# Narrowing float64 weights by integer bit operations on VectorE and ScalarE in a fused attention and gated feed-forward kernel

## The chip, the cores and the metric

One core of one Trainium2 chip runs the whole program. The metric is the device time of one launch in microseconds, the lower the better. The kernel before took 374.76 us (median of three runs, 373.27 to 375.42).

## The reference

```
a = S1 @ x, b = S2 @ x per token and head           # x is q or k, r = 8
phi(x) = outer(a, b), flattened to 64 features
kv = sum_s phi(k) v^T,  z = sum_s phi(k)
attn = (phi(q) @ kv) / (phi(q) . z + 1e-6)           # batch 4, heads 4, seq 1088, head_dim 32
x = attn as 4352 tokens x 128
out = (sigmoid(x @ w_gate) * (x @ w_val)) @ w_out    # d_ff 1536
```

q, k, v are float32. S1, S2 and the three weight matrices are float64: numpy's division and product by a float64 scalar make them so. They reach the chip as pairs of 32-bit words (low, high), and the kernel itself makes float32 of them.

## The kernel before, in words

The feed-forward part (called moe in the code) works on chunks of 512 tokens (`tok_chk`, eight of 512 and one of 256) and on twelve blocks of 128 hidden units (`NJ` = 12). For one chunk and one block, `w1` (L281) issues a **wave**: the gate and the value product into one PSUM tile (L292), a sigmoid on ScalarE (ACT, L300), and, emitted with the next wave, the product of the two on VectorE (DVE, L305, `glu`). `w2` (L246) multiplies the result of a block with w_out into the accumulator `moeout` (L252), some two waves later. There are 102 waves: twelve for each of the eight chunks of 512 tokens, and six of two blocks each for the last chunk.

The attention of batch 0 is computed ahead of the first wave as far as the first chunk needs it. All else of the attention (groups of matmuls for the feature maps `ab`, `kps`, `kv`, `den`, `num`) is put between the waves by `slot` (L319): a slot is one group and then one or two waves. The order on TensorE (PE), DVE, ACT and GpSimd (POOL) is the order in which the program text emits the instructions; each engine works through its own queue in that order. Loads are issued by SyncE (SP), each queued behind the waits of the ones ahead of it.

PSUM is tight: waves and the `aps` half of `ab` share two buffers (`psm`). Where an `ab` stands between two waves, the second of them takes the buffer of the first, and so waits for that wave's `glu` on DVE.

The first chunk is special: its twelve waves each need a new block of weights, and a block is narrowed just ahead. `load_w` (L135) loads two blocks of all three matrices into one `raw` buffer; `narrow_w(j)` (L156) narrows block j of the three matrices at once, 128 partitions x 384 values, into `w_sb`. Blocks 0 to 2 are narrowed ahead of wave 0, and wave j of the first chunk emits `narrow_w(j + 3)` ahead of its matmuls (L288). `narrow` (L81) makes, for one block:

- on DVE four integer operations: `head` (sign, exponent, upper mantissa; L94, L98), `power` (L101) and `ex` (L104);
- on ACT one copy of the low words to float, `rest` (L109);
- on POOL six operations: rest x power, + head, two comparisons of the exponent, their sum, and the last product, which writes `w_sb` (L110, L111, L113, L114, L117, L118).

The same `narrow` also treats S1 and S2 (`sr`, 128 x 64 values) at the start of the program; the feature matrices `sk`, `sa` and `sb` (L226 to L232) come from it, and every matmul of the attention needs one of them.

Of the kernel before, what the change touches and what calls it, by code (L numbers as in the profile page):

```python
# [8 lines left out]
F32 = mybir.dt.float32  # L9
I32 = mybir.dt.int32  # L10
U32 = mybir.dt.uint32
I64 = mybir.dt.int64
ALU = mybir.AluOpType
ACTF = mybir.ActivationFunctionType
MUL = ALU.mult
# [5 lines left out]
def kernel(  # L21
# [12 lines left out]
    nc = tc.nc  # L34
# [6 lines left out]
    NJ = DFF // P  # L41
    assert DM == H * D == P and D == 32 and R == 8 and S % 32 == 0

    T = S // 32
# [7 lines left out]
    const = ctx.enter_context(tc.tile_pool(name="const", bufs=1))  # L52
    ld = ctx.enter_context(tc.tile_pool(name="ld", bufs=2))
    sbA = ctx.enter_context(tc.tile_pool(name="sbA", bufs=2))
    raw = ctx.enter_context(tc.tile_pool(name="raw", bufs=3))
    sbN = ctx.enter_context(tc.tile_pool(name="sbN", bufs=2))
    sbG = ctx.enter_context(tc.tile_pool(name="sbG", bufs=6))

    psm = ctx.enter_context(tc.tile_pool(name="psm", bufs=2, space=bass.MemoryType.PSUM))
# [14 lines left out]
    q_chk = [(0, 9), (9, TP - 9)]  # L74
    T0 = 2 * q_chk[0][1]

    # float64 arrays arrive as int64 bit patterns, float32 ones as they are.
    wide = S1.dtype == I64
    assert all((a.dtype == I64) == wide for a in (S2, moe_w_gate, moe_w_val, moe_w_out))

    def narrow(out, bits):  # L81
        """out = the nearest float32 of the float64 in bits, pairs of words (low, high).

        Below float32's normal range it gives 0, beyond its largest value inf or NaN."""
        n, m = out.shape[1:]
        lo, hi = bits[:, :, :, 0].bitcast(U32), bits[:, :, :, 1]

        def tmp(dt, tag):
            return sbN.tile([P, 3, P], dt, tag=tag, name=tag)[:, :n, :m]

        head, power, ex = tmp(I32, "head"), tmp(I32, "power"), tmp(I32, "ex")
        rest, ok, big = tmp(F32, "rest"), tmp(F32, "ok"), tmp(F32, "big")
        # head: sign, exponent and the 20 mantissa bits of the high word, as a float32.
        nc.vector.tensor_scalar(  # L94
            out=head, in0=hi, scalar1=3, scalar2=0x3FFFFFF8,
            op0=ALU.logical_shift_left, op1=ALU.bitwise_and,
        )
        nc.vector.scalar_tensor_tensor(  # L98
            out=head, in0=hi, scalar=-0x40000000, in1=head, op0=ALU.bitwise_and, op1=ALU.bitwise_or
        )  # L100
        nc.vector.tensor_scalar(  # L101
            out=power, in0=head, scalar1=-0x800000, scalar2=None, op0=ALU.bitwise_and
        )
        nc.vector.tensor_scalar(  # L104
            out=ex, in0=hi, scalar1=20, scalar2=0x7FF,
            op0=ALU.logical_shift_right, op1=ALU.bitwise_and,
        )
        # rest: the low word's share, low * 2^-52 * (+-2^exponent).
        nc.scalar.activation(out=rest, in_=lo, func=ACTF.Copy, scale=2.0**-52)  # L109
        nc.gpsimd.tensor_tensor(out=rest, in0=rest, in1=power.bitcast(F32), op=MUL)  # L110
        nc.gpsimd.tensor_tensor(out=rest, in0=rest, in1=head.bitcast(F32), op=ALU.add)  # L111
        # The factor for the exponent: 0 too small, 1 in range, huge too large.
        nc.gpsimd.tensor_scalar(out=ok, in0=ex, scalar1=896.5, scalar2=None, op0=ALU.is_ge)  # L113
        nc.gpsimd.tensor_scalar(  # L114
            out=big, in0=ex, scalar1=1150.5, scalar2=3e38, op0=ALU.is_ge, op1=MUL
        )
        nc.gpsimd.tensor_tensor(out=ok, in0=ok, in1=big, op=ALU.add)  # L117
        nc.gpsimd.tensor_tensor(out=out, in0=rest, in1=ok, op=MUL)  # L118

    sr = const.tile([P, 2, D], F32, tag="sr", name="sr")  # L120
    sr_in = const.tile([P, 2, D, 2], I32, tag="sr_in", name="sr_in") if wide else None
    for n, s_ in enumerate((S1, S2)):
        rows = bass.AP(tensor=s_.tensor, offset=s_.offset, ap=[[0, P // R], [D, R], [1, D]])
        if wide:
            nc.scalar.dma_start(
                out=sr_in[:, n].rearrange("p d w -> p (d w)"), in_=rows.bitcast(I32)
            )
        else:
            nc.scalar.dma_start(out=sr[:, n], in_=rows)

    # w_sb[:, 0] = w_gate, [:, 1] = w_val (rows: model), [:, 2] = w_out (rows: within block j).
    w_sb = const.tile([P, 3, NJ, P], F32, tag="w_sb", name="w_sb")
    w_in = {}

    def load_w(n):  # L135
        j0, j1 = 2 * n, 2 * n + 2
        cs = slice(j0 * P, j1 * P)
        if wide:
            w_in[n] = raw.tile([P, 3, 2, P, 2], I32, tag="w_in", name="w_in")
        for i, src in enumerate((moe_w_gate, moe_w_val)):  # L140
            if wide:
                nc.sync.dma_start(
                    out=w_in[n][:, i].rearrange("p j m w -> p (j m w)"),
                    in_=src[:, cs].bitcast(I32),
                )
            else:
                nc.sync.dma_start(
                    out=w_sb[:, i, j0:j1].rearrange("p j m -> p (j m)"), in_=src[:, cs]
                )
        src = moe_w_out[cs, :].bitcast(I32) if wide else moe_w_out[cs, :]  # L150
        nc.sync.dma_start(
            out=w_in[n][:, 2].rearrange("p j m w -> p j (m w)") if wide else w_sb[:, 2, j0:j1],
            in_=src.rearrange("(j p) m -> p j m", p=P),
        )

    def narrow_w(j):  # L156
        n, jj = divmod(j, 2)
        if wide:
            narrow(w_sb[:, :, j, :], w_in[n][:, :, jj])
        if jj == 1 and n + 3 < NJ // 2:  # L160
            load_w(n + 3)

    # Column 32 t + i of a head is its token i T + t: 32 partitions a head, T tokens each.
    def load_rows(src, b, tag, parts=((0, T),)):
        t = ld.tile([P, T, D], F32, tag=tag, name=tag)
        for t0, t1 in parts:
            nc.sync.dma_start(
                out=t[:, t0:t1, :],
                in_=bass.AP(
                    tensor=src.tensor,  # L170
                    offset=src[b, 0].offset + t0 * D,
                    ap=[[T * D, P], [1, (t1 - t0) * D]],
                ),
            )
        return t
# [17 lines left out]
    k_t[0] = load_rows(k, 0, "k", halves)  # L193
    q_t[0] = load_rows(q, 0, "q", halves)
    v_t[0] = load_v(0)
    for n in range(3):
        load_w(n)

    def load_batch(b):
# [4 lines left out]

    load_batch(1)

    if wide:
        narrow(sr, sr_in)
    ones = const.tile([P, 32], F32, tag="ones")
    nc.vector.memset(ones, 1.0)  # L210

    sig0 = const.tile([P, 1], F32, tag="sig0")
    nc.scalar.activation(out=sig0, in_=ones[:, :1], func=ACTF.Sigmoid)
    ident = const.tile([P, P], F32, tag="ident")
    make_identity(nc, ident)

# [7 lines left out]
    for n, inner in enumerate(([[1, R], [0, R]], [[0, R], [1, R]])):  # L224
# [3 lines left out]
        t = const.tile([P, R, R], F32, tag=f"s{n}", name=f"s{n}")  # L228
        nc.scalar.copy(
            out=t, in_=bass.AP(tensor=st_.tensor, offset=st_.offset, ap=[list(st_.ap[0])] + inner)  # L230
# [6 lines left out]
    for n in range(2):  # L237
        t = const.tile([P, H, 32], F32, tag=f"zb{n}", name=f"zb{n}")
# [42 lines left out]
    def w1():  # L281

        ci = moe["ci"]
        t0, tw = tok_chk[ci]
        jn = TCH // tw
        j0 = moe["w"] * jn
        wv = psm.tile([P, 2, TCH], F32, tag="wave", name="wave")
        if ci == 0 and j0 + 3 < NJ:  # L288
            narrow_w(j0 + 3)
        for which in range(2):  # L290
            for jj in range(jn):
                nc.tensor.matmul(  # L292
                    out=wv[:, which, jj * tw : (jj + 1) * tw],
                    lhsT=w_sb[:, which, j0 + jj, :],
                    rhs=xT[:, t0 : t0 + tw],
                    start=True,
                    stop=True,
                )
        sg = sbG.tile([P, TCH], F32, tag="sg", name="sg", bufs=3)
        nc.scalar.activation(out=sg, in_=wv[:, 0], func=ACTF.Sigmoid)  # L300

        # Emitted with the next wave, so that the vector engine need not wait for the sigmoid.
        def glu():
            g = sbG.tile([P, TCH], F32, tag="g", name="g")
            nc.vector.tensor_tensor(out=g, in0=wv[:, 1], in1=sg, op=MUL)  # L305
            moe["todo"].append((ci, j0, jn, g.rearrange("p (j t) -> p j t", j=jn)))

        moe["gate"] = glu
        moe["w"] += 1
        if j0 + jn == NJ:  # L310
            moe["ci"] += 1
            moe["w"] = 0
# [41 lines left out]
    def turn_q(b, n):  # L354
        if b >= B:
            return
        if n == 0:
            qT_of[b] = sbA.tile([P, TP, 2, 32], F32, tag="qT", name="qT")
        t0, tn = q_chk[n]
        nc.vector.transpose(  # L360
            out=qT_of[b][:, t0 : t0 + tn].rearrange("p t c s -> p (t c s)"),
            in_=q_t[b][:, 2 * t0 : 2 * (t0 + tn)].rearrange("p t d -> p (t d)"),
        )
# [225 lines left out]
    invert()  # L589
    divide()  # L590
    narrow_w(2)
    turn_q(0, 1)

    def r_group(a_of, b_of):
# [83 lines left out]
```

## Time and profile before

| what | value |
|---|---|
| time, median of three runs | 374.76 us (373.27 to 375.42) |
| span of the profiled execution | 371.5 us |
| the profiled execution's own time | not listed apart; its span lies 3.3 us under the median |
| PE busy | 323.0 us (87%) |
| DVE busy | 172.5 us (46%) |
| POOL busy | 86.2 us (23%) |
| ACT busy | 80.6 us (22%) |

How to read it: the span goes from the first to the last instruction of the program, and what the runs take beyond it lies around the program. Busy shares are means over the whole span. Here they hide two stages: in the first 107 us PE has gaps and POOL is always busy; after that PE is always busy and POOL never. So the stages have to be looked at one by one. "Granted clock" is what TensorE got: 1.00 is 2.4 GHz and 0.50 is 1.2 GHz.

### The profile page before, as it was taken

The page shows a single profiled execution, that of the slowest core. Times are in us where ns is not written, and L with a number is a line of the kernel's source. Part 1 is how long each engine was busy: PE and PEld are TensorE (multiplying, and loading weights), DVE is VectorE, ACT ScalarE, POOL GpSimd, SP SyncE. Part 2 cuts the span into 40 slices and gives each one's busy share as a digit, 9 for nine tenths or more (in the row PEclk, how much of TensorE's full clock was granted, in tenths as well). Part 3 has the DMA queues.
Part 4 walks back from the last instruction along what each step waited for, and adds up shares of the span by engine and source line. Part 5 has one row for each costly group of instructions (what it writes and reads, how often), then busy time and mean ns, then how long its engine had stood idle before and what let it go on. Part 6 is the DMA issues. An engine that isn't in the chain of part 4 may idle for free.

```text
span 371.5 us, 3973 instructions
## 1 busy us (share of the span) xinstructions
PE 323.0 (87%) x1552; PEld 139.3 (37%) x1552; DVE 172.5 (46%) x294; ACT 80.6 (22%) x140; POOL 86.2 (23%) x86
## 2 busy tenths in 40 slices
PE   0735876675779999999999999999999999999994
PEld 0312222221323344343343434444444444444583
DVE  1886565699237654545742454222222322322321
ACT  3112112111212122221222111212222122221220
POOL 1179999999950000000000000000000000000000
PEclk9986788788699999999999999999999999999998
DMA  8960353110011000100001001000100100010010
GB/s 197 349 169 12 135 150 59 60 52 10 18 48 28 2 1 2 22 8 0 2 3 27 0 0 19 11 0 0 29 1 0 30 0 0 11 19 0 2 28 14
DMA packets 25587, 14.09 MB, mean 38 GB/s; under 512 B 19168, under 2 KB 22752, under 8 KB 25568
## 3 DMA queue, kind: packets, MB, share of 16 engines
q1 hardware_dynamic: 25280, 13.77, 14.7%
q8 instruction: 12, 0.20, 0.2%
q10 hardware_dynamic: 288, 0.07, 0.1%
q14 instruction: 7, 0.06, 0.1%
HBM read 11.60 MB, written 2.23 MB: 37 GB/s over the span
## 4 chain that ended last, share of the span: by engine, by line
PE 70%; POOL 21%; DVE 4%; issue 1%; DMA 1%; ACT 1%; POOLq 0%; ACTq 0%
PE wave L292 42%; PE moeout L252 22%; POOL big L114 5%; POOL ok L113 4%; POOL rest L110 3%; POOL rest L111 3%; POOL w_sb L118 3%; POOL ok L117 3%; DMA sr_in<-in_S_dram 1%; PE aps L414 1%; PE dps L515 1%; PE nps L550 1%; PE kps L372 1%; PE kvz L451 1%; DVE kp L391 1%
## 5 line engine op out<-in xcount | busy, mean ns | idle before, releaser
L292 PE MATMUL wave<-xT,w_sb 128*128 128x512 f32 (+1 forms) x432 | 200.8, 593 | 19.4 <-POOL w_sb L118 9.8
L305 DVE TENSOR_TENSOR g<-wave,sg 128x512 f32<-128x512 f32 x102 | 70.0, 686 | 130.9 <-ACT sg L300 130.9
L292 PEld LDWEIGHTS wave<-xT,w_sb 128*128 128x128 f32 x432 | 83.6, 197 | 120.9 <-issue 85.9
L252 PE MATMUL moeout<-g,w_sb 128*128 128x512 f32 (+1 forms) x216 | 109.6, 600 | 0.6 <-DVE g L305 0.6
L300 ACT ACTIVATE sg<-wave 128x512 f32<-128x512 f32 x102 | 60.8, 596 | 204.8 <-PE wave L292 204.8
L252 PEld LDWEIGHTS moeout<-g,w_sb 128*128 128x128 f32 x216 | 38.8, 194 | 44.1 <-issue 40.1
L433 DVE TENSOR_TENSOR qp<-bps,asb 128x576 f32<-128x576 f32 (+1 forms) x16 | 11.4, 720 | 22.0 <-PE bps L414 17.0
L109 ACT ACTIVATE rest<-w_in 128x384 f32<-128x384 uint32 x12 | 6.5, 553 | 61.9 <-POOL w_sb L118 61.9
L114 POOL TENSOR_SCALAR big<-ex 128x384 f32<-128x384 int32 (+1 forms) x13 | 18.6, 1434 | 0.8
L414 PE MATMUL aps<-qT,s 32*64 32x288 f32 (+1 forms) x128 | 13.2, 482 | 5.3 <-DVE g L305 2.9
L110 POOL TENSOR_TENSOR rest<-rest,power 128x384 f32<-128x384 f32 (+1 forms) x13 | 13.8, 1061 | 16.9 <-ACT rest L109 16.9
L372 PE MATMUL kps<-kT,sk 64*32 64x288 f32 x64 | 4.4, 548 | 14.5 <-DVE kT L348 14.5
L113 POOL TENSOR_SCALAR ok<-ex 128x384 f32<-128x384 int32 (+1 forms) x13 | 15.3, 1179 | 0.0
L391 DVE TENSOR_TENSOR kp<-kab 128x576 f32<-128x576 f32 (+2 forms) x20 | 14.5, 766 | 0.0
L111 POOL TENSOR_TENSOR rest<-rest,head 128x384 f32<-128x384 f32 (+1 forms) x13 | 13.4, 1028 | 1.0
L414 PE MATMUL bps<-qT,s 32*64 32x288 f32 (+1 forms) x128 | 13.0, 481 | 0.0
L117 POOL TENSOR_TENSOR ok<-ok,big 128x384 f32<-128x384 f32 (+1 forms) x13 | 12.4, 953 | 1.1
L118 POOL TENSOR_TENSOR w_sb<-rest,ok 128x384 f32<-128x384 f32 x12 | 12.3, 1029 | 0.9
L414 PEld LDWEIGHTS aps<-qT,s 32*64 32x64 f32 x128 | 4.0, 150 | 18.4 <-DVE qT L360 6.2
L424 ACT COPY asb<-aps 128x576 f32<-128x576 f32 (+1 forms) x16 | 9.8, 610 | 5.2 <-PE aps L414 3.7
L560 DVE TENSOR_TENSOR xT<-nps,rb 128x576 f32<-128x576 f32 (+1 forms) x8 | 5.8, 724 | 7.7 <-PE nps L550 7.6
L101 DVE TENSOR_SCALAR power<-head 128x384 int32<-128x384 int32 (+1 forms) x13 | 8.9, 681 | 0.5
(53 smaller groups left out, 118.2 us busy)
## 6 DMA issues: line engine op xcount, KB each, us to landing
v<-in_v_dram SPq DMA_DIRECT2D x16, 144.0 KB, 7.4
k<-in_k_dram SPq DMA_DIRECT2D x3, 544.0 KB, 6.3
q<-in_q_dram SPq DMA_DIRECT2D x3, 544.0 KB, 7.8
w_in<-in_moe_w_gate_dram SPq DMA_DIRECT2D x6, 256.0 KB, 4.1
w_in<-in_moe_w_val_dram SPq DMA_DIRECT2D x6, 256.0 KB, 4.3
w_in<-in_moe_w_out_dram SPq DMA_DIRECT2D x6, 256.0 KB, 5.6
out_dram<-o_sb SPq DMA_DIRECT2D x20, 64.0 KB, 2.0
k<-in_k_dram SPq DMA_DIRECT2D x1, 288.0 KB, 3.0
```

The costliest lines, as they stand in the source:

```text
L110: nc.gpsimd.tensor_tensor(out=rest, in0=rest, in1=power.bitcast(F32), op=MUL)
L111: nc.gpsimd.tensor_tensor(out=rest, in0=rest, in1=head.bitcast(F32), op=ALU.add)
L113: nc.gpsimd.tensor_scalar(out=ok, in0=ex, scalar1=896.5, scalar2=None, op0=ALU.is_ge)
L114: nc.gpsimd.tensor_scalar(out=big, in0=ex, scalar1=1150.5, scalar2=3e38, op0=ALU.is_ge, op1=MUL)
L117: nc.gpsimd.tensor_tensor(out=ok, in0=ok, in1=big, op=ALU.add)
L118: nc.gpsimd.tensor_tensor(out=out, in0=rest, in1=ok, op=MUL)
L252: nc.tensor.matmul(out=moe["acc"][:, :tw], lhsT=w_sb[:, 2, j, :], rhs=g[:, jj, :tw], start=(j == 0), stop=(j == NJ - 1),)
L292: nc.tensor.matmul(out=wv[:, which, jj * tw : (jj + 1) * tw], lhsT=w_sb[:, which, j0 + jj, :], rhs=xT[:, t0 : t0 + tw], start=True, stop=True,
L300: nc.scalar.activation(out=sg, in_=wv[:, 0], func=ACTF.Sigmoid)
L305: nc.vector.tensor_tensor(out=g, in0=wv[:, 1], in1=sg, op=MUL)
L391: nc.vector.tensor_tensor(out=KP[b][:, h, j0:j1].rearrange("p j (i l) -> p j i l", i=R), in0=bass.AP(tensor=a0.tensor, offset=a0.offset, a ...
L414: nc.tensor.matmul(out=dst[64 * c : 64 * c + 64, m, : 32 * tn], lhsT=sx[rows, :], rhs=qT_of[bb][rows, t0 : t0 + tn, c, :], start=True, sto ...
```

## The change

The steps of `narrow` are other ones, they run on other engines, and its last step is emitted later.

```diff
-    raw = ctx.enter_context(tc.tile_pool(name="raw", bufs=3))
-    sbN = ctx.enter_context(tc.tile_pool(name="sbN", bufs=2))
+    raw = ctx.enter_context(tc.tile_pool(name="raw", bufs=4))
+    sbN = ctx.enter_context(tc.tile_pool(name="sbN", bufs=4))
...
-        head, power, ex = tmp(I32, "head"), tmp(I32, "power"), tmp(I32, "ex")
-        rest, ok, big = tmp(F32, "rest"), tmp(F32, "ok"), tmp(F32, "big")
...
+        cap, head, tail = tmp(I32, "cap"), tmp(I32, "head"), tmp(I32, "tail")
+        nc.vector.tensor_scalar(
+            out=cap.bitcast(F32), in0=hi.bitcast(F32), scalar1=122880.0, scalar2=-122880.0,
+            op0=ALU.min, op1=ALU.max,
+        )
+        nc.vector.tensor_scalar(
+            out=head, in0=cap, scalar1=3, scalar2=0x3FFFFFF8,
+            op0=ALU.logical_shift_left, op1=ALU.bitwise_and,
+        )
+        nc.vector.scalar_tensor_tensor(
+            out=head, in0=cap, scalar=-0x40000000, in1=head, op0=ALU.bitwise_and, op1=ALU.bitwise_or
+        )
+        nc.scalar.activation(out=tail, in_=lo, func=ACTF.Copy, scale=2.0**-29)
+        nc.scalar.activation(out=cap.bitcast(F32), in_=cap.bitcast(F32), func=ACTF.Square)
+        nc.gpsimd.tensor_tensor(out=head, in0=head, in1=tail, op=ALU.add)
+
+        def last():
+            nc.vector.scalar_tensor_tensor(
+                out=out, in0=cap.bitcast(F32), scalar=1.265625 * 2.0**-30, in1=head.bitcast(F32),
+                op0=ALU.is_ge, op1=MUL,
+            )
+
+        return last
...
-            nc.scalar.dma_start(
+            nc.sync.dma_start(
                 out=sr_in[:, n].rearrange("p d w -> p (d w)"), in_=rows.bitcast(I32)
             )
...
-        if jj == 1 and n + 3 < NJ // 2:
-            load_w(n + 3)
+        if jj == 1 and n + 4 < NJ // 2:
+            load_w(n + 4)
...
-    for n in range(3):
+    for n in range(4):
         load_w(n)
...
-    if wide:
-        narrow(sr, sr_in)
...
     nc.scalar.activation(out=sig0, in_=ones[:, :1], func=ACTF.Sigmoid)
+    if wide:
+        narrow(sr, sr_in)()
...
-        if ci == 0 and j0 + 3 < NJ:
-            narrow_w(j0 + 3)
+        if ci == 0:
+            if j0 + 3 < NJ:
+                narrow_w(j0 + 3)
+            narrow_last(j0 + 1)
...
     narrow_w(2)
+    narrow_last(0)
```

For one block there are now three operations on DVE (`cap`, and `head` twice), two on ACT (`tail`, and the square of `cap`), one integer add on POOL, and a last operation on DVE that writes `w_sb`. `narrow_w` keeps that last one, and `narrow_last(j)` emits it: for block j + 1 with wave j, so two waves after the block's first steps.

On DVE around wave 0 (`xT` is the attention's output, `w_in` and `w_sb` the weights before and after narrowing, `g` the output of `glu`), in the program before:

```order
L560 TENSOR_TENSOR xT<-nps,rb 128x2x9x32
L94 TENSOR_SCALAR head<-w_in 128x384
L98 SCALAR_TENSOR_TENSOR head<-w_in,head 128x384
L101 TENSOR_SCALAR power<-head 128x384
L104 TENSOR_SCALAR ex<-w_in 128x384
L360 STREAM_TRANSPOSE qT<-q 128x512
```

and in the changed one, whose line numbers differ:

```order
L568 TENSOR_TENSOR xT<-nps,rb 128x2x9x32
L94 TENSOR_SCALAR cap<-w_in 128x384
L99 TENSOR_SCALAR head<-cap 128x384
L103 SCALAR_TENSOR_TENSOR head<-cap,head 128x384
L113 SCALAR_TENSOR_TENSOR w_sb<-cap,head 128x3x128
L368 STREAM_TRANSPOSE qT<-q 128x512
```

So the write of `w_sb` has come from POOL to DVE, and the one for wave 0 stands behind the first three steps of block 2.

On ACT around the first waves (`asb` is the copy of the `aps` half of a group of the attention, `sg` the sigmoid), before:

```order
L109 ACTIVATE rest<-w_in 128x384
L300 ACTIVATE sg<-wave 128x512
L424 COPY asb<-aps 128x2x256
L109 ACTIVATE rest<-w_in 128x384
L300 ACTIVATE sg<-wave 128x512
```

and now:

```order
L107 ACTIVATE tail<-w_in 128x384
L108 ACTIVATE cap<-cap 128x384
L308 ACTIVATE sg<-wave 128x512
L432 COPY asb<-aps 128x2x256
L107 ACTIVATE tail<-w_in 128x384
L108 ACTIVATE cap<-cap 128x384
L308 ACTIVATE sg<-wave 128x512
```

Each sigmoid now has the square of a block's `cap` ahead of it, which waits for that block's three steps on DVE.

SP's queue begins, in the changed program, with S1 and S2, which ACT issued before:

```order
L125 DMA sr_in<-in_S_dram 128x1x64 x2
L173 DMA k<-in_k_dram 128x576
L173 DMA k<-in_k_dram 128x512
L173 DMA q<-in_q_dram 128x576
L173 DMA q<-in_q_dram 128x512
```

Behind these come v, now four pairs of blocks of weights instead of three, and then the loads of batch 1.

## Rows read from the trace of the kernel before

**Rows 1.** The chain that ended last, share of the span by engine

```profile
PE 70%; POOL 21%; DVE 4%; issue 1%; DMA 1%; ACT 1%; POOLq 0%; ACTq 0%
```

**Rows 2.** Stretches: busy of PE, PEld, DVE, ACT, POOL; granted clock; DMA share, GB/s

```profile
27.79:107.44 79.65, 53.70 (x272) 18.44 (x273) 51.95 (x77) 14.52 (x28) 76.27 (x66) 0.78 0.22 63
90.00:100.00 10.00, 7.96 (x54) 2.85 (x55) 4.91 (x9) 2.11 (x4) 9.54 (x9) 0.50 0.00 0
107.44:371.50 264.06, 258.96 (x1062) 115.91 (x1062) 103.62 (x172) 60.01 (x101) 0.00 (x0) 1.00 0.06 9
```

**Rows 3.** Timeline of POOL, first block and last write: start, us, what

```profile
20.51 1.00 POOL L110 TENSOR_TENSOR rest<-rest,power 128x384 f32<-128x384 f32 x1 [9.86 <-ACT rest L109]
21.59 1.19 POOL L111 TENSOR_TENSOR rest<-rest,head 128x384 f32<-128x384 f32 x1
...
24.08 1.50 POOL L114 TENSOR_SCALAR big<-ex 128x384 f32<-128x384 int32 x1
...
106.39 0.99 POOL L118 TENSOR_TENSOR w_sb<-rest,ok 128x384 f32<-128x384 f32 x1
```

**Rows 4.** Timeline of PE: the gate and value products of three waves

```profile
27.79 3.78 PE L292 MATMUL wave<-xT,w_sb 128*128 128x512 f32 x4 [1.81 <-POOL w_sb L118]
...
107.44 1.98 PE L292 MATMUL wave<-xT,w_sb 128*128 128x512 f32 x4 [2.43 <-POOL w_sb L118]
...
137.32 1.88 PE L292 MATMUL wave<-xT,w_sb 128*128 128x512 f32 x4
```

**Rows 5.** Waits from 28 to 107.5: total us, times, longest

```profile
ACT rest L109 <- POOL w_sb L118: 61.9, 10, 7.3
...
PE wave L292 <- POOL w_sb L118: 9.8, 5, 3.3
...
PE wave L292 <- ACT asb L424: 9.6, 4, 4.4
```

**Rows 6.** Timeline of the queues of ACT and SP: S1 and S2, then q

```profile
0.71 1.28 ACTq L125 DMA_DIRECT2D sr_in<-in_S_dram  x2
...
1.64 1.09 SPq L167 DMA_DIRECT2D q<-in_q_dram  x2
```

**Rows 7.** Transfers: KB each, median us from issue to landing

```profile
q<-in_q_dram SPq DMA_DIRECT2D x1, 288.0 KB, 5.6
...
sr_in<-in_S_dram ACTq DMA_DIRECT2D x2, 32.0 KB, 3.8
```

**Rows 8.** Timeline of DVE, ahead of wave 0

```profile
11.92 0.73 DVE L360 STREAM_TRANSPOSE qT<-q 128x576 f32<-128x576 f32 x1
...
18.32 0.54 DVE L94 TENSOR_SCALAR head<-w_in 128x384 int32<-128x384 int32 x1
18.90 0.56 DVE L98 SCALAR_TENSOR_TENSOR head<-w_in,head 128x384 int32<-128x384 int32 x1
19.49 0.36 DVE L101 TENSOR_SCALAR power<-head 128x384 int32<-128x384 int32 x1
...
20.81 1.11 DVE L98 SCALAR_TENSOR_TENSOR head<-w_in,head 128x384 int32<-128x384 int32 x1
21.96 1.03 DVE L101 TENSOR_SCALAR power<-head 128x384 int32<-128x384 int32 x1
...
23.37 0.33 DVE L506 COPY zb<-ndps 64x4 f32<-64x4 f32 x2
...
26.81 0.76 DVE L560 TENSOR_TENSOR xT<-nps,rb 128x576 f32<-128x576 f32 x1
```

**Rows 9.** DVE groups by shape: busy us, mean ns, idle before

```profile
L101 DVE TENSOR_SCALAR power<-head 128x384 int32<-128x384 int32 x12 | 8.7, 722 | 0.4
L98 DVE SCALAR_TENSOR_TENSOR head<-w_in,head 128x384 int32<-128x384 int32 x12 | 7.7, 645 | 0.4
L104 DVE TENSOR_SCALAR ex<-w_in 128x384 int32<-128x384 int32 x12 | 6.5, 546 | 4.9 <-POOL big L114 4.9
L94 DVE TENSOR_SCALAR head<-w_in 128x384 int32<-128x384 int32 x12 | 6.5, 541 | 1.4 <-POOL rest L111 1.4
```

More of the change, by code (lines that the diff above doesn't have):

```diff
@@ L89, in tmp @@
             return sbN.tile([P, 3, P], dt, tag=tag, name=tag)[:, :n, :m]
-        head, power, ex = tmp(I32, "head"), tmp(I32, "power"), tmp(I32, "ex")
-        rest, ok, big = tmp(F32, "rest"), tmp(F32, "ok"), tmp(F32, "big")
+        cap, head, tail = tmp(I32, "cap"), tmp(I32, "head"), tmp(I32, "tail")
         nc.vector.tensor_scalar(
-            out=head, in0=hi, scalar1=3, scalar2=0x3FFFFFF8,
+            out=cap.bitcast(F32), in0=hi.bitcast(F32), scalar1=122880.0, scalar2=-122880.0,
[3 more added lines that the diff above has]
+            out=head, in0=cap, scalar1=3, scalar2=0x3FFFFFF8,
             op0=ALU.logical_shift_left, op1=ALU.bitwise_and,
@@ L98, in narrow @@
         nc.vector.scalar_tensor_tensor(
-            out=head, in0=hi, scalar=-0x40000000, in1=head, op0=ALU.bitwise_and, op1=ALU.bitwise_or
+            out=head, in0=cap, scalar=-0x40000000, in1=head, op0=ALU.bitwise_and, op1=ALU.bitwise_or
         )
[L101 to L118, printed above, removed]
+        nc.scalar.activation(out=tail, in_=lo, func=ACTF.Copy, scale=2.0**-29)
[7 more added lines that the diff above has]
+        return last
     sr = const.tile([P, 2, D], F32, tag="sr", name="sr")
@@ L128 @@
         else:
-            nc.scalar.dma_start(out=sr[:, n], in_=rows)
+            nc.sync.dma_start(out=sr[:, n], in_=rows)
     w_sb = const.tile([P, 3, NJ, P], F32, tag="w_sb", name="w_sb")
@@ L154, in load_w @@
         )
+    narrowed = {}
     def narrow_w(j):
@@ L158, in narrow_w, with narrow_last @@
         if wide:
-            narrow(w_sb[:, :, j, :], w_in[n][:, :, jj])
-        if jj == 1 and n + 3 < NJ // 2:
-            load_w(n + 3)
+            narrowed[j] = narrow(w_sb[:, :, j, :], w_in[n][:, :, jj])
+        if jj == 1 and n + 4 < NJ // 2:
+            load_w(n + 4)
+    def narrow_last(j):
+        if j in narrowed:
+            narrowed.pop(j)()
     def load_rows(src, b, tag, parts=((0, T),)):
```

## The prediction

> **What bounds the kernel now.** I read the chain that ended last first. It lies on PE for 70% of the span and on POOL for 21% [rows 1]; an engine that does no matmul holds a fifth of the time. The busy time by stretch says where [rows 2]. From 107.44 us on, PE is busy 258.96 of 264.06 us at a granted clock of 1.00 and POOL does nothing: that part is PE's own work. Between 27.79 and 107.44, POOL is busy 76.27 of 79.65 us, PE only 53.70, at a mean clock of 0.78.
>
> POOL's timeline tells why. Its first step for a block of weights starts at 20.51 and its last write of `w_sb` at 106.39 [rows 3]: twelve blocks of six operations, (106.39 + 0.99 - 20.51) / 12 = 7.24 us a block. Wave 0 starts at 27.79 and wave 11, the last one that needs a new block, at 107.44, and both are released by POOL's write of `w_sb` [rows 4]. So the first chunk's waves come at POOL's pace, and what else was late there was late through it: ACT waited 61.9 us for POOL to give its buffers back, PE 9.8 us directly, and 9.6 us for copies on ACT that stood behind that wait [rows 5].
>
> So the time is: start of wave 11, plus 264 us in which PE is always busy, plus the edges. The change can only move the start of wave 11, since the slots behind it keep their order.
>
> **The sum: up to wave 0.** S1 and S2 now go first on SP. Their two issues took ACT 1.28 us, and SP issued the first half of q at 1.64 [rows 6]. The median transfer of S1 and S2 took 3.8 us, that half of q 5.6 [rows 7]; so q landed at about 7.2, where DVE turned it only at 11.92 [rows 8], behind work that needs `sr` from POOL. With the two issues ahead of it on SP, q lands at about 8.5. S1 and S2 are there by 0.7 + 1.3 + 3.8 = 5.8 and need one small add on POOL instead of six steps, so q is the later of the two, and DVE turns it 11.92 - 8.5 = 3.4 us earlier. Bounds: nothing, if the loads behind it set the pace of the attention's first steps; and 4.7 us, if q lands as early as before. I take 3.5, since the rows on q are the nearest.
>
> The narrowing of blocks 0 and 1 stands on DVE ahead of the attention's last steps: from 18.32 to 23.37, 5.05 us for eight operations, two of which were stretched while POOL worked [rows 8]. Now there are six, with POOL idle until the first add: 0.54 + 0.36 + 0.56 and small gaps make 1.55 us a block, 3.1 for two, a gain of 2.0. `xT` is then finished at 26.81 + 0.76 - 5.5 = 22.1. But wave 0 no longer waits for POOL: its `w_sb` is written by DVE behind three steps of block 2, 1.55 + 0.65 us. Wave 0 starts at 24.3, that is 3.5 us earlier.
>
> **Wave 0 to wave 11.** DVE was busy 51.95 us there [rows 2]. Of it go the four old operations of ten blocks, 0.722 + 0.645 + 0.546 + 0.541 = 2.45 us each [rows 9], so 24.5. What stays is 27.5 us of attention and `glu`. New: nine blocks (3 to 11) of three steps at 1.6 us (each between its value alone, as above, and its mean beside POOL, since one add is left) = 14.4, and eleven last operations, which are of the form of L98, at 0.65 = 7.2. Together 49 us of DVE work in place of 52: DVE does as much as before, without POOL's pace over it.
>
> PE's own work there: behind wave 11 nine slots of the same kind took 137.32 - 107.44 = 29.88 us with PE never idle, 3.32 us each [rows 4]; eleven slots are 36.5 us at 2.4 GHz, 46.8 us at a clock of 0.78, 73 at 1.2 GHz. So DVE and PE are about equally loaded, and they wait for each other: a wave behind an `ab` needs the `glu` of the wave before, that `glu` the sigmoid, and the sigmoid now has a `cap` square ahead of it on ACT, which waits for three steps on DVE. These waits no row shows. Below, they are nothing; above, the stage is PE's 73 us at half clock. The nearest row is PE's 9.6 us behind ACT's copies [rows 5]; I take 7, as ACT no longer waits for POOL. 49 + 7 = 56 us in place of 79.65.
>
> POOL's add, between 1.0 and 1.2 us [rows 3] for a block that now takes some 5, is hidden; ACT's second operation lies in its idle time (busy 14.52 of 79.65 us [rows 2]) but for the order just named. The fourth `raw` buffer moves three loads ahead of batch 1's, whose first use is behind wave 2: hidden. The loads of batch 2 keep their place behind the weights, which now get their buffers earlier: hidden too.
>
> Wave 11 starts at 24.3 + 56 = 80.3 instead of 107.44: 27 us less. The span of 371.5 becomes 344.4, and the median of 374.76, which lies 3.3 us above it, **347.7 us**.
>
> **A rule that speaks against it.** One row of L98 took 0.56 us with POOL idle and the next 1.11 beside it, L101 0.36 and 1.03 [rows 8]. The Trainium skill ("Advanced Engine Details and Errata", VectorE Performance Modes) says that the second Vector port is shared with GpSimd, so that such instructions block each other; the trace agrees. The new last operation is of just this kind and it runs on the engine that now sets the pace. If every add holds DVE for all of its own time, that is 11 x 1.1 = 12 us where my sum has some 2.5 (0.65 against 0.56, 1.6 against 1.46): 347.7 + 9.5 = 357.2 us. It is a rival below.
>
> **The rivals.**
> 1. *DVE alone sets the pace, nothing waits.* Wave 11 at 24.3 + 49 = 73.3, or 71 with shorter operations: 338 to 341 us. For it: DVE's queue has work in nearly every slot. Against: the chain from `glu` to `glu` through PSUM.
> 2. *PE stays at 1.2 GHz.* In the stretch from 90 to 100 the granted clock was 0.50 although PE was busy 7.96 of 10 us [rows 2]. At half clock throughout, wave 11 starts at 24.3 + 73 = 97.3: 364.6 us. Against: PE works more densely than before, and it got 0.78 even so. By the skill's "TensorE: Matmul & The Clock Gate" (Part 1), idle time throttles and activity releases the clock, which fits the 1.00 of the unbroken stretch.
> 3. *The shared port*, as above: 357.2 us.
> 4. *Nothing is gained ahead of the attention* (S1 and S2 on SP delay k, q and v as much as they help): 351 us.
> 5. *Slower: the int32 add.* No row shows an add of two int32 tensors on POOL. The nearest are a float add of 1.19 us and an operation with an int32 input of 1.50 [rows 3]; a price below these changes nothing, as it is hidden. If it took a path many times as long, POOL would set the pace again: its adds start near 16.3 (18.32 - 3.5 + 1.5), so it decides from (106.4 - 16.3) / 12 = 7.5 us an add. At 9 us wave 11 starts at about 125.5, and the time is 393 us. Only an eightfold price does it.
>
> **How the numbers follow.** My forecast 0.60; DVE alone 0.10; half clock 0.08; the port 0.12; no early gain 0.07; slow add 0.03. The range reaches from 338 (no waits) to 360 (the port and some waits more): it leaves out the half clock, the slow add, and the outer edge of the others. A measurement of this kernel tells a change of about 0.5%, here 1.9 us, from none. All cases but the last are faster than 372.9; 0.02 for a sum of them that eats the gain.
>
> **What would show it.** In the changed profile: POOL busy some 15 us instead of 86; wave 0 at 24 us and wave 11 near 80; between them DVE busy about 49 of 56 us; no wait of ACT for POOL; behind wave 11 again 264 us of PE without a gap. Wrong it would be if waves 0 to 11 still come 7 us apart (then some queue's order took POOL's place), if wave 0 does not move, or if PE gets gaps behind wave 11.

## The result, and the profile after

The changed kernel takes **342.0 us** (median of four runs, 341.1 to 344.4); the kernel before took 375.1 us beside it. The ratio is 0.914, 95% interval 0.910 to 0.919. The forecast was 347.7 us, range 338 to 360.

The chain that ended last, after (share of the span by engine), to be held against [rows 1]:

```profile
PE 83%; DVE 10%; DMA 2%; issue 2%; ACT 1%; SPq 1%; DVEq 0%
```

POOL is gone from it; what it held has become PE's, and DVE's where it holds PE up. Waves 0 to 2 and wave 11 on PE's timeline, after (start, us; compare [rows 4]):

```profile
24.90 3.78 PE L300 MATMUL wave<-xT,w_sb 128*128 128x512 f32 x4 [4.05 <-DVE w_sb L113]
30.44 3.78 PE L300 MATMUL wave<-xT,w_sb 128*128 128x512 f32 x4 [0.70 <-ACT asb L432]
35.85 1.88 PE L300 MATMUL wave<-xT,w_sb 128*128 128x512 f32 x4
...
78.77 1.88 PE L300 MATMUL wave<-xT,w_sb 128*128 128x512 f32 x4
```

Wave 0 starts 2.9 us earlier than before, wave 11 28.7 us earlier. The same stretches as in [rows 2], after: between the two waves, its first slots, and all that follows (busy of PE, PEld, DVE, ACT, POOL, then granted clock, DMA share, GB/s):

```profile
24.90:78.77 53.87, 44.41 (x272) 15.90 (x273) 41.79 (x74) 18.34 (x37) 11.46 (x10) 0.88 0.34 96
24.90:36.00 11.10, 10.40 (x35) 3.56 (x36) 5.77 (x12) 4.68 (x10) 3.19 (x3) 0.57 1.04 284
...
78.77:342.60 263.83, 258.85 (x1063) 115.89 (x1062) 104.77 (x174) 59.97 (x101) 0.00 (x0) 1.00 0.06 9
```

Behind wave 11 nothing changed: 263.83 us against 264.06. The whole gain lies ahead of it: 79.65 us from wave 0 to wave 11 became 53.87. DVE's narrowing and POOL's add, after, by shape (busy us, mean ns, idle before):

```profile
L103 DVE SCALAR_TENSOR_TENSOR head<-cap,head 128x384 int32<-128x384 int32 x12 | 6.7, 559 | 0.4
L113 DVE SCALAR_TENSOR_TENSOR w_sb<-cap,head 128x384 f32<-128x384 f32 x12 | 6.6, 551 | 0.0
L94 DVE TENSOR_SCALAR cap<-w_in 128x384 f32<-128x384 f32 x12 | 6.4, 537 | 0.2 <-DMA w_in<-in_moe_w_out_dram 0.2
...
L99 DVE TENSOR_SCALAR head<-cap 128x384 int32<-128x384 int32 x12 | 4.3, 360 | 0.4
```

```profile
L109 POOL TENSOR_TENSOR head<-head,tail 128x384 int32<-128x384 int32 x12 | 13.8, 1154 | 51.1 <-DVE head L103 38.2 <-ACT tail L107 12.9
```

The int32 add takes 1.15 us, as the float add did (1.19 in [rows 3], 1.09 in the mean of its twelve), and POOL now waits for DVE instead of being waited for. DVE's narrowing steps have the lengths that they had before with POOL idle [rows 8]: 0.54, 0.36, 0.56.

### The profile page after: what moved, and what is told of

Read it like the earlier page. It is cut to its first block, busy times and chain, and to the rows that moved or that the text cites. A ratio compares the mean times of both kernels' runs of the same rounds, so it can differ in the third digit from the quotient of the medians.

```text
span 342.6 us, 3915 instructions
## 1 busy us (share of the span) xinstructions
PE 314.2 (92%) x1552; PEld 137.8 (40%) x1552; DVE 163.3 (48%) x294; ACT 85.1 (25%) x152; POOL 15.0 (4%) x21
## 4 chain that ended last, share of the span: by engine, by line
PE 83%; DVE 10%; DMA 2%; issue 2%; ACT 1%; SPq 1%; DVEq 0%
PE wave L300 49%; PE moeout L258 25%; PE aps L422 3%; PE kvz L459 2%; DMA q<-in_q_dram 2%; DVE g L313 1%; PE dps L523 1%; DVE head L103 1%; DVE cap L94 1%; PE nps L558 1%; DVE w_sb L113 1%; PE bps L422 1%; DVE head L99 1%; DVE kp L399 1%; DVE qT L368 1%
## 5 line engine op out<-in xcount | busy, mean ns | idle before, releaser
L300 PE MATMUL wave<-xT,w_sb 128*128 128x512 f32 (+1 forms) x432 | 195.7, 581 | 6.0 <-DVE w_sb L113 4.8
L258 PE MATMUL moeout<-g,w_sb 128*128 128x512 f32 (+1 forms) x216 | 107.4, 590 | 1.8 <-DVE g L313 1.8
L441 DVE TENSOR_TENSOR qp<-bps,asb 128x576 f32<-128x576 f32 (+1 forms) x16 | 11.4, 720 | 22.9 <-PE bps L422 17.9
L109 POOL TENSOR_TENSOR head<-head,tail 128x384 int32<-128x384 int32 (+1 forms) x13 | 14.1, 1089 | 55.3 <-DVE head L103 42.4
L108 ACT ACTIVATE cap<-cap 128x384 f32<-128x384 f32 (+1 forms) x13 | 6.5, 502 | 29.4 <-DVE head L103 29.4
L459 PE MATMUL kvz<-kp,v 128*32 128x64 f32 (+1 forms) x288 | 8.8, 246 | 0.2 <-DVE kp L399 0.2
L459 PEld LDWEIGHTS kvz<-kp,v 128*32 128x32 f32 (+1 forms) x288 | 6.3, 124 | 6.2 <-issue 4.0
L103 DVE SCALAR_TENSOR_TENSOR head<-cap,head 128x384 int32<-128x384 int32 (+1 forms) x13 | 6.9, 533 | 0.5
L368 DVE STREAM_TRANSPOSE qT<-q 128x576 f32<-128x576 f32 (+1 forms) x8 | 5.9, 736 | 1.7 <-DMA q<-in_q_dram 1.7
L268 DVE STREAM_TRANSPOSE o_sb<-moeout 128x512 f32<-128x512 f32 (+1 forms) x9 | 6.1, 676 | 1.2 <-PE moeout L258 1.2
L107 ACT ACTIVATE tail<-w_in 128x384 int32<-128x384 uint32 x12 | 6.6, 553 | 0.0
```

The costliest lines, as they stand in the source:

```text
L103: nc.vector.scalar_tensor_tensor(out=head, in0=cap, scalar=-0x40000000, in1=head, op0=ALU.bitwise_and, op1=ALU.bitwise_or)
L109: nc.gpsimd.tensor_tensor(out=head, in0=head, in1=tail, op=ALU.add)
L258: nc.tensor.matmul(out=moe["acc"][:, :tw], lhsT=w_sb[:, 2, j, :], rhs=g[:, jj, :tw], start=(j == 0), stop=(j == NJ - 1),)
L300: nc.tensor.matmul(out=wv[:, which, jj * tw : (jj + 1) * tw], lhsT=w_sb[:, which, j0 + jj, :], rhs=xT[:, t0 : t0 + tw], start=True, stop=True,
L368: nc.vector.transpose(out=qT_of[b][:, t0 : t0 + tn].rearrange("p t c s -> p (t c s)"), in_=q_t[b][:, 2 * t0 : 2 * (t0 + tn)].rearrange("p ...
L441: nc.vector.tensor_tensor(out=QP[bb][:, 2 * pr : 2 * pr + 2, 32 * t0 : 32 * t0 + w], in0=bps[:, :, :w], in1=ASB[b_of][:, :, :w], op=MUL,)
```

## The experiments

All ratios are to the kernel before on the same chip. The changed kernel was run twice: 0.914 (0.910 to 0.919) as above, and once more beside later experiments, 0.912 (0.909 to 0.915).

**What of the change did it.** First, the kernel before with POOL's part cut short:

```diff
-        nc.gpsimd.tensor_tensor(out=rest, in0=rest, in1=head.bitcast(F32), op=ALU.add)
+        nc.gpsimd.tensor_tensor(out=out, in0=rest, in1=head.bitcast(F32), op=ALU.add)
...
-        nc.gpsimd.tensor_scalar(out=ok, in0=ex, scalar1=896.5, scalar2=None, op0=ALU.is_ge)
...
-        nc.gpsimd.tensor_tensor(out=out, in0=rest, in1=ok, op=MUL)
```

> The kernel before, with POOL's part of the narrowing cut to its first two steps (low words times power, plus head); the comparisons of the exponent, which guard values outside float32's range, are left out. DVE's four steps, ACT's copy, the buffers and the order of the loads stay. Theory: POOL's six steps at 7.2 us a block were the pace; with about 2.2 us a block the waves come at the pace of DVE and PE as in the changed kernel, and only the early gain of S1 and S2 on SP is missing: 343 to 350 us. Rival: the four buffers and the late last step were needed for it: 357 us or more.

345.5 us (345.0 to 348.3), ratio 0.923 (0.919 to 0.926). Its POOL groups:

```profile
L111 POOL TENSOR_TENSOR w_sb<-rest,head 128x384 f32<-128x384 f32 x12 | 13.4, 1118 | 0.9
L110 POOL TENSOR_TENSOR rest<-rest,power 128x384 f32<-128x384 f32 x12 | 12.0, 999 | 36.6 <-DVE power L101 24.1 <-ACT rest L109 11.5 <-ACT sg L293 1.0
```

POOL, with 2.1 us a block (1.118 and 0.999), idles 36.6 us, mostly for DVE. Nothing but four POOL operations a block has gone, and some 30 of the 33 us have gone with them. The pace was POOL's.

Then the fourth buffer alone, in the kernel before:

```diff
-    raw = ctx.enter_context(tc.tile_pool(name="raw", bufs=3))
+    raw = ctx.enter_context(tc.tile_pool(name="raw", bufs=4))
...
-        if jj == 1 and n + 3 < NJ // 2:
-            load_w(n + 3)
+        if jj == 1 and n + 4 < NJ // 2:
+            load_w(n + 4)
...
-    for n in range(3):
+    for n in range(4):
         load_w(n)
```

> The kernel before with a fourth raw buffer, and so with the fourth pair of blocks loaded ahead of batch 1. Theory: POOL's pace hides when the weights come: within 1.5 us of 375. Rival: the loads of weights were late in places: 2 us less or more.

374.8 us, ratio 0.999 (0.996 to 1.002): nothing, as the theory had it.

And the changed kernel with S1 and S2 issued by ACT again:

```diff
-            nc.sync.dma_start(
+            nc.scalar.dma_start(
                 out=sr_in[:, n].rearrange("p d w -> p (d w)"), in_=rows.bitcast(I32)
```

> S1 and S2 are issued by ACT again, all else as in the changed kernel (342.0 us, wave 0 at 24.9 us of its span, the first turn of q at 9.3). Theory: the early gain came from the shorter narrowing of S1 and S2, and the turn of q waits for q's transfer; with SP free 1.3 us earlier q lands at about 8 and S1, S2 at 5.8, so wave 0 moves by less than 1 us either way: 341 to 343 us. Rival: the order on SP made the early gain: wave 0 comes some 3 us later, 345 us.

345.4 us (343.7 to 347.5), ratio 0.921 (0.916 to 0.926). DVE's timeline in this run, with wave 0 on PE's, and then DVE's in the changed kernel:

```profile
6.78 0.20 DVE L94 TENSOR_SCALAR cap<-sr_in 128x64 f32<-128x64 f32 x1 [5.88 <-DMA sr_in<-in_S_dram]
...
10.61 0.74 DVE L368 STREAM_TRANSPOSE qT<-q 128x576 f32<-128x576 f32 x1
...
27.08 3.78 PE L300 MATMUL wave<-xT,w_sb 128*128 128x512 f32 x4 [3.55 <-DVE w_sb L113]
```

```profile
3.73 0.20 DVE L94 TENSOR_SCALAR cap<-sr_in 128x64 f32<-128x64 f32 x1 [2.83 <-DMA sr_in<-in_S_dram]
...
9.32 0.78 DVE L368 STREAM_TRANSPOSE qT<-q 128x576 f32<-128x576 f32 x1 [1.67 <-DMA q<-in_q_dram]
```

My theory said within 1 us, and it falls: wave 0 came at 27.08 instead of 24.90, 2.2 us later, so the rival is nearer. Issued by ACT beside SP's k and q, S1 and S2 reached DVE at 6.8 us; issued on SP ahead of them, at 3.7. That is the place of most of the early gain. Its size is known less well: each run has one trace, and in the six traces in which DVE does the same ahead of wave 0 with S1 and S2 first on SP (the changed kernel twice, and four runs that follow) wave 0 starts between 23.54 and 25.35. The time's own difference of 3 us is not clear of the first run of the changed kernel, whose interval overlaps this one, but is of the second.

This run and the one with four POOL operations less can be held against each other. Both issue S1 and S2 on ACT; one has all of the new steps, the later last step and the fourth buffer, the other has the old steps less four: 0.921 and 0.923, not to be told apart. So the new steps, with the last one emitted late, are worth in time what leaving out the four operations is worth. What it adds is that values outside float32's range are still guarded, by the min and max of `cap` and the comparison in the last step, which the shortened old kernel leaves out.

**Who sets the pace now.** The first step on DVE three times for every block:

```diff
-        nc.vector.tensor_scalar(
-            out=cap.bitcast(F32), in0=hi.bitcast(F32), scalar1=122880.0, scalar2=-122880.0,
...
+        for _ in range(3):
+            nc.vector.tensor_scalar(
+                out=cap.bitcast(F32), in0=hi.bitcast(F32), scalar1=122880.0, scalar2=-122880.0,
...
```

> Each block's first step on DVE is done three times instead of once, 2 x 0.55 us more for each of twelve blocks; the value is the same. Theory: DVE's queue sets the pace, so nearly all of 13 us shows: 351 to 356 us. Rival: PE at its granted clock sets it, and only the three blocks ahead of wave 0 show in full (3.3 us) and half of the rest: 347 to 350 us.

353.4 us (352.8 to 356.0), ratio 0.943 (0.939 to 0.946): 11.4 us for 13 us of added work. From wave 0 to wave 11:

```profile
27.69:87.52 59.83, 46.61 (x273) 16.56 (x273) 51.49 (x92) 18.23 (x37) 11.46 (x10) 0.85 0.27 75
```

Wave 0 itself came 2.8 us later than 24.90, and the stage is 6.0 us longer than 53.87 (8.8 longer than the 51.02 of the changed kernel's second trace, below). So nearly all of DVE's added work shows, though DVE (third of the busy times) is busy in only 51.49 of 59.83 us here, and in 41.79 of 53.87 us of the changed kernel. The mean hides the reason: in the changed kernel DVE is busy 33.70 of the 36.35 us from 35.19 to 71.54; its waits lie mostly ahead of that and behind it. The two largest in the changed kernel between wave 0 and wave 11 (total, times, longest):

```profile
DVE qp L441 <- PE bps L422: 6.0, 2, 3.2
...
DVE g L313 <- ACT sg L308: 3.3, 2, 2.0
```

The last step at once, instead of two waves later:

```diff
-            narrowed[j] = narrow(w_sb[:, :, j, :], w_in[n][:, :, jj])
+            narrow(w_sb[:, :, j, :], w_in[n][:, :, jj])()
```

> The write of w_sb on DVE stands right behind the other steps of its block, and so DVE waits for ACT's tail and POOL's add each time. Theory: DVE sets much of the pace up to wave 11, and each of the twelve waits (about 1.3 us from the third step to the end of the add) holds the queue behind it: 10 to 16 us more, 352 to 358 us. Rival: DVE, busy 41.8 of 53.9 us there, has room for it: at most 5 us more, 347 us or less.

353.4 us (352.9 to 355.0), ratio 0.942 (0.939 to 0.945). One row of its waits (total, times, longest):

```profile
DVE w_sb L113 <- POOL head L109: 11.7, 10, 1.2
```

11.4 us more, and DVE waits 11.7 us for POOL's add from 25 to 86 us, for ten of the twelve blocks: putting that step off is worth a third of the gain, in this kernel and with POOL's other steps gone.

Narrowing left out but for a copy on ACT:

```diff
-            narrowed[j] = narrow(w_sb[:, :, j, :], w_in[n][:, :, jj])
+            nc.scalar.activation(out=w_sb[:, :, j, :], in_=w_in[n][:, :, jj, :, 0].bitcast(U32),
+                                 func=ACTF.Copy, scale=2.0**-36)
```

> The narrowing of the twelve blocks is left out but for one copy of the low words on ACT, which fills w_sb; S1 and S2 are narrowed as in the changed kernel. Theory: DVE's work for the narrowing (24 us) is what the first chunk waits for: wave 0 comes near 20, the stage to wave 11 nears PE's own 36.5 us, and the time is 322 to 328 us. Rival: the waits between PE, ACT and DVE keep the stage near 50 us whatever DVE has to do: 334 us or more.

327.6 us (326.8 to 328.8), ratio 0.873 (0.870 to 0.876). Its stretch from wave 0 to wave 11:

```profile
21.39:61.16 39.77, 39.22 (x273) 14.92 (x274) 22.34 (x36) 14.17 (x26) 0.00 (x0) 0.95 0.52 144
```

PE is busy 39.22 of 39.77 us, at a mean clock of 0.95: this is PE's floor for these slots. The changed kernel stands 11 to 14 us above it in this stage. This run leaves out DVE's steps together with ACT's square and POOL's add; that it is DVE's steps that cost rests on the tripled step above, which showed nearly in full, and on the two runs below, in which ACT's order cost nothing and twelve more adds on POOL a few us at most.

**What waits for what.** ACT's two steps and POOL's add behind the sigmoid (`narrow` returns them as a step of its own, here `rest`):

```diff
-                narrow_w(j0 + 3)
+                rest = narrow_w(j0 + 3)
...
         nc.scalar.activation(out=sg, in_=wv[:, 0], func=ACTF.Sigmoid)
+        if ci == 0 and j0 + 3 < NJ:
+            rest()
```

> ACT's two steps for block j + 3 (and with them POOL's add) stand behind the sigmoid of wave j instead of ahead of it. Theory: the sigmoid's wait for the square, which waits for three steps on DVE, is a part of the waits between wave 0 and wave 11: 2 to 4 us less than the changed kernel. Rival: the sigmoid waits for its wave anyway and the square is done by then: within 1 us, or 1 to 2 us more, as the copies behind it on ACT come later.

342.3 us (340.0 to 343.9), ratio 0.911 (0.908 to 0.914), and beside it the changed kernel once more:

> The changed kernel once more, on the chip and among the runs of the next three. Expected: 341 to 345 us, ratio 0.909 to 0.919, with a spread of some 3 us between its executions. Theory on the spread: the granted clock falls to 1.2 GHz at other waves of the first chunk in each execution; rival: it comes from the loads at the start.

342.4 us (340.4 to 344.9), ratio 0.912 (0.909 to 0.915). So the order on ACT costs nothing that can be measured, and the rival holds. The second trace of the changed kernel shows one source of its spread. Waves 0 and 1, and the stretch from wave 0 to wave 11:

```profile
25.35 3.52 PE L300 MATMUL wave<-xT,w_sb 128*128 128x512 f32 x4 [3.55 <-DVE w_sb L113]
30.16 1.98 PE L300 MATMUL wave<-xT,w_sb 128*128 128x512 f32 x4 [0.70 <-ACT asb L432]
```

```profile
25.35:76.37 51.02, 41.80 (x273) 15.15 (x274) 41.78 (x74) 18.25 (x37) 11.47 (x10) 0.97 0.34 99
```

DVE's work is the same to 0.01 us, but the mean clock is 0.97 instead of 0.88, wave 1 takes 1.98 instead of 3.78, and the stage 51.02 instead of 53.87. The loads cannot have done that: wave 0 came no earlier. But the clock is not all of the spread: the executions at 344.4 and 341.1 us of the first run both had a mean clock of 0.979, and the fastest of the second, 340.4 us, had 0.983 where this one, at 342.0, had 0.993. The loads at the start, the rival, are another source, as far as single traces show: in the trace of the run with ACT's steps behind the sigmoid, whose work ahead of wave 0 is the same, DVE turned q at 7.51 without waiting for it, instead of at 8.62 and 9.32 in the changed kernel's two, and wave 0 started at 23.77.

**The shared port.** Two integer adds a block on POOL, each with half of the low words:

```diff
-        nc.scalar.activation(out=tail, in_=lo, func=ACTF.Copy, scale=2.0**-29)
+        nc.scalar.activation(out=tail, in_=lo, func=ACTF.Copy, scale=2.0**-30)
...
         nc.gpsimd.tensor_tensor(out=head, in0=head, in1=tail, op=ALU.add)
+        nc.gpsimd.tensor_tensor(out=head, in0=head, in1=tail, op=ALU.add)
```

> POOL adds the low words in two halves: two integer adds of 1.15 us a block instead of one. Theory: the add lies beside other work and two waves ahead of its use: within 1 us of 342.0. Rival (the port that DVE shares with POOL): every add holds DVE for most of its time, so twelve more cost 6 to 12 us: 348 to 354 us.

344.4 us (342.5 to 346.7), ratio 0.918 (0.913 to 0.922). The rival's 6 to 12 us are out. What the second add costs, between nothing and some 5 us (from 0.909 to 0.922), stays open; the medians differ by 2. Three of DVE's steps here:

```profile
L103 DVE SCALAR_TENSOR_TENSOR head<-cap,head 128x384 int32<-128x384 int32 x12 | 7.4, 615 | 0.4
L114 DVE SCALAR_TENSOR_TENSOR w_sb<-cap,head 128x384 f32<-128x384 f32 x12 | 7.2, 601 | 0.0
...
L99 DVE TENSOR_SCALAR head<-cap 128x384 int32<-128x384 int32 x12 | 5.0, 419 | 0.4
```

They took 0.05 to 0.06 us more each in the mean: 2.0 us over twelve blocks. The mean is of a few long ones: L99 took up to 1.06 us, but 0.36 in the median. DVE is busy 44.54 us from wave 0 to wave 11 instead of 41.79. So the second add meets DVE's steps now and then, not every time.

The one add of the changed kernel is not free either, though its narrowing steps keep their lengths. It meets three steps of the attention. The first of the sums for batch 1, in the changed kernel beside the add, and in the run with the narrowing left out, where POOL is idle in this stage:

```profile
63.36 1.18 POOL L109 TENSOR_TENSOR head<-head,tail 128x384 int32<-128x384 int32 x1 [6.07 <-DVE head L103]
63.60 2.02 DVE L493 TENSOR_TENSOR z<-kp 128x1024 f32<-128x1024 f32 x1
...
L493 DVE TENSOR_TENSOR z<-kp 128x1024 f32<-128x1024 f32 x1 | 1.2, 1206 | 0.0
```

With one of four outer products (1.56 us, the others 0.74 to 0.75) and one small step (0.41 instead of 0.17) that makes 1.9 us in all.

**A faster version.** PE waits for DVE ahead of wave 0, and the clock is then at 1.2 GHz for the first wave or two. Three matmuls without use, into the PSUM tile that wave 0 then overwrites, fill that wait:

```diff
+        if ci == 0 and j0 == 0:
+            for _ in range(3):
+                nc.tensor.matmul(
+                    out=wv[:, 0], lhsT=ident, rhs=kT_of[0][:, :TCH], start=True, stop=True
+                )
```

> Three matmuls of 128x512 without use are put on PE ahead of wave 0, into the PSUM tile that wave 0 overwrites, while PE waits for DVE (from about 21 to 24.9 us). Theory: waves 0 and 1 ran at 1.2 GHz (3.78 us instead of 1.9) because PE had idled ahead of them; with them at 2.4 GHz the time falls by 2 to 3 us and the executions agree better. Rival: DVE sets the pace of these slots, and the clock there costs nothing: within 1 us.

**339.8 us** (339.0 to 341.1), ratio 0.905 (0.903 to 0.907), clear of the changed kernel's 0.912 (0.909 to 0.915) beside it. PE's timeline (each float32 matmul is two records):

```profile
20.11 4.07 PE L296 MATMUL wave<-kT,ident 128*128 128x512 f32 x6
24.02 1.88 PE L305 MATMUL wave<-xT,w_sb 128*128 128x512 f32 x4
27.42 1.98 PE L305 MATMUL wave<-xT,w_sb 128*128 128x512 f32 x4 [0.94 <-ACT asb L437]
```

Waves 0 and 1 take 1.9 and 2.0 us, and wave 2 starts 6.90 us behind wave 0 instead of 8.31 and 10.95 in the changed kernel's two traces. Useless work that made the kernel faster: the clock was the price of the idle time. That the executions agree better is not shown: these lie 2.0 us apart instead of 4.5, but in the two runs that follow, with the same three matmuls, 3.4.

Last, on top of these matmuls, DVE's sums for batch 1 on POOL; the second run does the same for one outer product (`h == 3`):

```diff
+        eng = nc.gpsimd if b == 1 else nc.vector
...
-        nc.vector.tensor_tensor(out=z4, in0=kp[:, :, 1:5], in1=kp[:, :, 5:9], op=ALU.add)
+        eng.tensor_tensor(out=z4, in0=kp[:, :, 1:5], in1=kp[:, :, 5:9], op=ALU.add)
...
```

> The three matmuls without use ahead of wave 0 stay (339.8 us), and the sums over tokens of batch 1 (3.0 us of DVE's work between waves 7 and 8) go to POOL, which is idle there but for its adds. Theory: DVE's queue sets the pace of that slot, which took 7.1 us: 2 to 3 us less, 336.5 to 338 us. Rival: POOL is slower and shares a port with DVE, so that DVE's own steps and the sums come as late as before: within 1 us of 339.8, or more.

> As the run above, and one of the four outer products of batch 1 (0.8 us on DVE) goes to POOL too. Theory: another 0.5 to 1 us less than the run above. Rival: that product is now behind POOL's adds and the matmuls that need it wait: 1 to 2 us more than the run above.

339.6 us (337.5 to 341.0), ratio 0.905 (0.902 to 0.908), and 339.3 us (338.0 to 341.4), ratio 0.905 (0.901 to 0.908): no gain from either. DVE and POOL in the first of them, while POOL sums:

```profile
59.44 2.41 POOL L499 TENSOR_TENSOR z<-kp 128x1024 f32<-128x1024 f32 x1
...
60.41 1.66 DVE L99 TENSOR_SCALAR head<-cap 128x384 int32<-128x384 int32 x1
...
61.93 1.26 POOL L500 TENSOR_TENSOR z<-z 128x512 f32<-128x512 f32 x1
62.10 1.50 DVE L103 SCALAR_TENSOR_TENSOR head<-cap,head 128x384 int32<-128x384 int32 x1
...
63.53 1.08 DVE L113 SCALAR_TENSOR_TENSOR w_sb<-cap,head 128x384 f32<-128x384 f32 x1
```

The three steps take 1.66, 1.50 and 1.08 us instead of 0.36, 0.56 and 0.55: 2.8 us lost. What left DVE is 3.6 us of sums by the trace of the run above (2.02, 0.69, 0.42 and 0.42), and not the 3.0 that I had expected; the 0.8 between them is less than these intervals can tell.

## Why the prediction was right, step by step

- *POOL's pace bounds the first chunk.* Right, and shown: without four of POOL's six operations a block the kernel before is 30 us faster; with more buffers alone it is no faster. (POOL was busy from 20.5 us on, and not in all of the first 107 us, as I wrote under the time before.)
- *Up to wave 0.* Forecast 24.3, measured 24.90. The reason was half right. q did gate the turn, at 9.32 where I had 8.5, and the steps behind it came as summed. But the order on SP, which I had counted as a cost to q, is what brought S1 and S2 to DVE at 3.7 instead of 6.8 us, and some 2 us of the 2.9 hang on it. I had them at 5.8 and thought that early enough, counting one add behind them; from S1 and S2 to q's turn DVE needs 3.8 us (6.78 to 10.61 with S1 and S2 on ACT). At 5.8 they, and not q, would have set the turn, at about 9.6. That q came last was luck.
- *Wave 0 to wave 11.* Forecast 56 us, measured 53.87, and 51.02 in the second trace. The sum was near by luck: two errors met. DVE's work I put at 49 us; it is 41.79. What stays on DVE I had at 27.5; it is 41.79 less 9 x 1.456 and 11 x 0.551, that is 22.6, and 22.34 where nothing is narrowed there. The new steps I had at 21.6; they are the other 19.2. Some 3 of the first 4.9 us are that the attention's steps of before were stretched beside POOL's work, which was to go: the four outer products took 1.46 us each and take 0.95, and the last three sums took 1.37, 1.10 and 0.60 and take 0.69, 0.42 and 0.42. The rest is one more turn of q in the old stretch, and that the steps' lengths, which I took from a busy time, overlap by a little. The waits, in turn, I put at 7 us; DVE idles 12, and 9 in the second trace. And they are not the sigmoid's wait for the square, as I had it: moved behind the sigmoid, nothing is gained. They are waits for PE and for the sigmoid behind a wave, as the rows above show, and a part of them is the price of the clock: the one of 3.2 us ends at 35.19, behind the two waves at 1.2 GHz, and is 0.83 in the second trace.
- *Behind wave 11* the same 264 us: right.
- *The edges.* I set the profiled execution 3.3 us under the median and kept that distance. After, the profiled execution itself has 344.4 us for a span of 342.6, so 1.8 us lie around the span. By that, the profiled execution before, with its span of 371.5, was the one of 373.27 us, the fastest of its three, and the rest of the 3.3 was its distance from the median. Of the 5.7 us between 347.7 and 342.0, 1.8 are the span (344.4 against 342.6), 1.5 the edges, and 2.4 the profiled execution's place above its median.
- *The rivals.* DVE alone without waits: no, it idles 9 to 12 us. Half clock throughout: no, 0.88 and 0.97. The slow add: no, 1.15 us. No early gain: no, 2.9 us. The shared port: for the adds some 1.9 us of DVE's time in the changed kernel, where the rival had 9.5 on top of my sum; and it is not the new last operation that pays, which keeps its 0.55 us, but three steps of the attention. The Trainium skill's rule ("Advanced Engine Details and Errata", VectorE Performance Modes), that GpSimd and those VectorE instructions that use the second port block each other, holds all the same: where POOL has longer two-input work, DVE's step goes from 0.36 to 1.66 us.

## What to carry to other kernels

Durations read beside a busy neighbour are not those that remain when the neighbour goes: take them from stretches in which it is idle. An engine whose chain paces a stage is best relieved of steps, not given more buffers; and a step that needs another engine's result belongs a turn or two later in its queue. An idle engine is no free place for two-input work if it shares a port with the one that sets the pace.

## What the runs showed that I had not expected

Three matmuls without use, put into a wait of PE, saved 2.6 us (342.4 to 339.8), because PE otherwise came out of that wait at a granted clock of 1.2 GHz: 0.57 is the mean of the stretch from 24.90 to 36.00 above. And two small transfers of 32 KB reached DVE 3.1 us earlier when they stood ahead of the larger ones on SP than when ACT issued them beside these, 3.73 instead of 6.78, though q then kept DVE waiting 1.67 us.
